# Stacked key halves from block 2 on, and block 0's first products of slices 8 to 15 from split weights and split tokens

## The chip, the cores and the metric

The kernel runs on one core of a Trainium2 chip. The metric is the device time of one execution in microseconds; before the change the median of three runs is 1127.58 us (1126.95 to 1127.78). The engines are TensorE (PE; its weight loads are listed as PEld), VectorE (DVE), ScalarE (ACT), GpSimd (POOL) and SyncE (SP), which issues most transfers. A difference of 0.2%, about 2.25 us, is the least that the measurement tells from no change.

## The reference

Three stages follow each other. Attention with 4 sink keys and a window of 128 (4 batches, 8 heads, 768 positions, 64 wide) gives 3072 tokens of 512 numbers. A dense layer pair follows, and then a mixture of 8 experts in which every token goes to its best one.

```python
x = attn_out.transpose(0, 2, 1, 3).reshape(B * S, H * D)   # 3072 x 512
h = np.maximum(x @ w_in, 0.0)                               # w_in 512 x 2048
x = h * h @ w_out                                           # w_out 2048 x 512
...
e_idx = np.argmax(x @ w_gate, axis=1)
for e in range(E):
    mask = e_idx == e
    h = np.maximum(x[mask] @ w1[e], 0.0)
    out[mask] = gate_w[mask, None] * eom[mask, e, None] * (h @ w2[e])
```

The weights of the dense pair come as float64.

## The kernel before, in words

The 3072 tokens are worked in 12 blocks of 256 (t = 0 to 11). For each block PE makes the dense pair in 16 slices of 128 hidden units (j): `l1(t, j)` is a slice's first product, from the tokens `x` and the weights `WI`, and `l2(t, j)` its second, into two accumulators. Between the two, ACT takes the positive part (line 692), POOL (block 0) or DVE squares it (line 699), ACT makes a high part of the square (line 701) and DVE the low part (line 702). The attention of block t + 1 is worked among the slices of block t, so that PE always has something to do; its pieces are `prep_k`, `prep_q` (transposed keys and queries), `scores`, `ptrans`, `pv` (weights times values), `fin_sink` and `add_sink` (the sink keys' share). Behind block 11 comes the expert stage.

Products of float32 numbers are made in one of two ways. In plain float32 the operands are used as they are. In the split way each operand is a high part in the reduced format fp32r and a low part (the rest), and three products high·high, high·low, low·high stand for one. A split costs an ACT copy for the high part and a DVE subtraction for the low part; `fin()` in `conv` does it for weights (lines 340 and 341).

Weights of the dense pair arrive as float64 in slabs of 512 KB, one for each slice of w_in and one for each slice of w_out, in turn. There are three slab buffers. `conv` turns a slab into float32: two passes on ACT (lines 327 and 330) and two on DVE (lines 336 and 337); the end of DVE's second pass frees the slab buffer, and SP issues the next load. The float32 slice (`fw`) lies in the place that the low part of the split slice will have. In block 0 the weights are still coming in: there the first products of all 16 slices, and the second products of slices 0 to 7, are plain float32 from `fw` (lines 682 and 711), and the split of those slices (`fins`) follows once they were used, by the rule of `LAGS` 12 or 13 slices later at the latest. `cstep` in the loop over slices starts the conversions ahead of the slices that need them.

`scores` works in three forms. Blocks 0 and 1 use plain float32 (line 521). Block 2 uses split queries and keys as three products for each of the two heads of a pair, each on 64 of the 128 rows (line 528), six in all. From block 3 on the keys are stacked: a head's high part on one half of the rows and its low part on the other, so that two products on all 128 rows do (line 524), four in all. For that `prep_k` and `prep_q` write each head's half by itself (lines 423, 425, 470, 472) and POOL copies query halves (line 474). The constant `STK` is the first block in the stacked form, `T32` the first in a split form.

The order of each engine's instructions is fixed when the kernel is built, by a scheduler that goes by program order, by priorities (`tc.high_priority`) and by its own estimates of durations; at run time each engine works through its list in order and waits on semaphores. `psH`, `psX`, `psS`, `psT`, `psO` are the pools of accumulators.

In the tables below psh is a first product's accumulator, psx a second product's, pss a unit of scores, pspt and PT its transposed probabilities, pso the product with the values, psst and psk the sink share, xT the split tokens, craw a slab, fw a float32 slice, h and r the hidden units.

## Time and profile before

| | us |
|---|---|
| median of 3 runs | 1127.58 |
| the profiled execution, its own time | 1127.6 |
| its span | 1125.9 |
| PE busy | 1103.8 (98%) |
| DVE busy | 777.6 (69%) |
| ACT busy | 667.6 (59%) |
| POOL busy | 448.9 (40%) |

The time of an execution is about 1.7 us longer than the span, which runs from the first to the last instruction. Busy shares are means over stages that differ: block 0 lies between about 38 and 123 us, block 1 ends at about 190 us, the dense pair ends at about 762 us, and the expert stage fills the rest. PE's ends are modelled and its instructions overlap, so the time that a group of products takes is read from the start of its first one to the start of what follows. An idle time in brackets names who released the engine.

### The profile page before, as it was taken

Reading aid. Unit: us, or ns where it says so; the run is one execution under the profiler, and the core shown is the slowest. Engines: PE = TensorE matmul, PEld = TensorE weight load, DVE = VectorE, ACT = ScalarE, POOL = GpSimd, SP = SyncE. Lnnn points to the kernel's source line nnn. Section 1 sums busy time; section 2 is a strip of 40 time slices with the busy share of each in tenths; the row PEclk is TensorE's granted clock in tenths of the full one; section 3 lists DMA queues with packets and bytes.
Section 4 is the critical chain, followed back from the end, with each engine's and each line's share of the span. In section 5 each row is a group of like instructions: output and inputs, shape, how many; then the busy total and the mean of one; then the engine's idle time right before and its main releaser. Section 6 shows DMA issues by size and latency. Waiting matters only on the chain. (4 is left out here: it accounts for less than half of the span.)

```text
span 1125.9 us, 23911 instructions
## 1 busy us (share of the span) xinstructions
PE 1103.8 (98%) x6858; PEld 938.7 (83%) x6858; DVE 777.6 (69%) x2094; ACT 667.6 (59%) x1821; POOL 448.9 (40%) x997
## 2 busy tenths in 40 slices
PE   9999999999999999999999999999999999999997
PEld 5556788989999989999988999997788888888886
DVE  6799877788887778787778787567412576864144
ACT  6788777778787878787877777454222222222200
POOL 3234564356664436576336665210211222221121
PEclk9999999999999999999999999999999999999999
DMA  6676211121111111211111110394411456654111
GB/s 163 181 219 196 72 26 49 40 56 37 52 29 50 39 49 35 57 30 48 39 51 38 39 32 2 60 233 158 132 39 48 162 178 227 218 193 153 48 46 34
DMA packets 139329, 100.09 MB, mean 89 GB/s; under 512 B 103843, under 2 KB 112163, under 8 KB 139174
## 3 DMA queue, kind: packets, MB, share of 16 engines
q1 hardware_dynamic: 131604, 83.19, 26.5%
q0 software_dynamic: 5408, 14.19, 3.7%
q8 instruction: 63, 1.03, 0.4%
q10 hardware_dynamic: 2162, 0.92, 0.3%
q14 instruction: 92, 0.75, 0.3%
HBM read 85.56 MB, written 13.76 MB: 88 GB/s over the span
## 5 line engine op out<-in xcount | busy, mean ns | idle before, releaser
L690 PE MATMUL psh<-xT,WI 128*128 128x256 f32 x2112 | 283.9, 283 | 0.6 <-ACT xT L649 0.6
L690 PEld LDWEIGHTS psh<-xT,WI 128*128 128x128 f32 x2112 | 265.7, 188 | 8.8 <-ACT xT L649 0.8
L1032 PE MATMUL psh<-WI,xt 128*128 (+1 forms) x672 | 162.1, 395 | 1.0 <-ACT xt L1012 0.7
L714 PE MATMUL psx<-WOb,h 128*128 128x512 f32 x576 | 151.4, 398 | 1.3 <-ACT h L701 0.9
L1032 PEld LDWEIGHTS psh<-WI,xt 128*128 128x128 f32 x672 | 123.8, 188 | 26.7 <-ACT xt L1012 1.4
L714 PE MATMUL psx<-WOa,h 128*128 128x512 f32 x528 | 139.0, 398 | 0.0
L699 DVE TENSOR_TENSOR r<-r 128x256 f32<-128x256 f32 x176 | 90.5, 515 | 59.5 <-ACT r L692 58.1
L1048 DVE TENSOR_TENSOR ht<-psht,ht 128x512 fp32r<-128x512 f32 x56 | 38.5, 689 | 120.8 <-ACT ht L1012 120.4
L714 PEld LDWEIGHTS psx<-WOb,h 128*128 128x128 f32 x576 | 101.6, 188 | 20.7 <-ACT h L701 2.3
L701 ACT ACTIVATE h<-r 128x256 fp32r<-128x256 f32 x184 | 76.3, 415 | 61.0 <-DVE r L699 54.7
L714 PEld LDWEIGHTS psx<-WOa,h 128*128 128x128 f32 x528 | 92.8, 188 | 15.1
L1070 POOL DMA_INDIRECT out_dram<-xg,pidx x28 | 29.4, 1049 | 190.4 <-ACT xg L1069 132.9
L702 DVE TENSOR_TENSOR h<-r,h 128x256 fp32r<-128x256 f32 x184 | 83.1, 451 | 23.1 <-ACT h L701 20.6
L581 POOL TENSOR_SCALAR_AFFINE_SELECT PT<-PT 128x256 fp32r<-128x256 f32 x224 | 96.8, 465 | 2.2 <-PE pss L528 1.2
L536 ACT ACTIVATE P<-P,st 128x260 f32<-128x260 f32 (+1 forms) x192 | 92.6, 485 | 7.0 <-DMA vn<-in_v_dram 3.5
L692 ACT ACTIVATE r<-psh 128x256 f32<-128x256 f32 x192 | 72.8, 379 | 34.2 <-PE psh L690 28.9
L1038 ACT ACTIVATE r<-psh 128x512 f32<-128x512 f32 x48 | 28.8, 599 | 98.8 <-PE psh L1032 94.5
L1061 PE MATMUL psy<-WOb,ht 128*128 (+1 forms) x336 | 84.0, 398 | 0.0
L617 POOL TENSOR_TENSOR xr<-tB,tC 128x128 f32<-128x128 f32 x80 | 37.0, 462 | 114.5 <-DVE tB L616 74.6
L1061 PE MATMUL psy<-WOa,ht 128*128 (+1 forms) x336 | 82.2, 392 | 0.0
L1003 POOL DMA_INDIRECT xg<-x2tab,pidx x30 | 42.2, 1407 | 90.7 <-issue 50.0
L533 DVE CUSTOM_DVE_ANT_0 P<-pss,M 128x260 f32<-128x260 f32 (+1 forms) x184 | 68.4, 398 | 10.6 <-POOL V L480 3.3
(459 smaller groups left out, 2108.5 us busy)
## 6 DMA issues: line engine op xcount, KB each, us to landing
raw<-in_moe_w_dram SPq DMA_DIRECT2D x36, 1024.0 KB
craw<-in_moe_w_out_dram SPq DMA_DIRECT2D x15, 512.0 KB
craw<-in_moe_w_in_dram SPq DMA_DIRECT2D x14, 512.0 KB
x2tab<-x2s SPq DMA_DIRECT2D x24, 256.5 KB
kn<-in_k_dram SPq DMA_DIRECT2D x64, 96.0 KB
vn<-in_v_dram SPq DMA_DIRECT2D x64, 96.0 KB
qn<-in_q_dram SPq DMA_DIRECT2D x92, 64.0 KB
kn<-in_k_dram SPq DMA_DIRECT2D x32, 64.0 KB
```

Of the source, the lines that this page charges most:

```text
L533: V.tensor_tensor_reduce(out=P[:, e, 0:W], in0=ps[e][:, 0:W], in1=mask[:, 0:W], scale=-SCALE, scalar=3.0e38, op0=ALU.add, op1=ALU.min, acc ...
L536: exps.append(A.activation(out=P[:, e, 0:W], in_=P[:, e, 0:W], func=AF.Exp, scale=-1.0, bias=st[:, e:e + 1], accum_out=st[:, 4 + e:5 + e]))
L581: G.affine_select(out=both[:, 1 - b, e], in_=bf[:, 0, e], pattern=[[0, 2], [1 - 2 * b, 128]], compare_op=ALU.is_gt if b else ALU.is_ge, fi ...
L690: PE.matmul(ps[:], lhsT=WI[:, j, a_, kk, :], rhs=x[:, b_, kk, :], start=(n == 0), stop=(n == 11))
L692: A.activation(out=hq[:], in_=ps[:], func=AF.Relu)
L699: E_.tensor_tensor(out=hq[:], in0=hq[:], in1=hq[:], op=ALU.mult)
L701: A.activation(out=o[:, 0], in_=hq[:], func=AF.Copy)
L702: V.tensor_tensor(out=o[:, 1], in0=hq[:], in1=o[:, 0].bitcast(F32), op=ALU.subtract)
L714: PE.matmul(acc[t][m][:], lhsT=o[:, a_, 128 * m:128 * m + 128], rhs=WO[j // 8][:, j % 8, b_, :], start=(j == 0 and n == 0), stop=(j == NF ...
L1003: G.indirect_dma_start(out=x, out_offset=None, in_=x2tab[:] if s >= PRE else x2tab[0:256 * (NBLK - 3)], in_offset=bass.IndirectOffsetOnAxi ...
L1032: PE.matmul(ps[:], lhsT=o[:, a_, kk, :], rhs=wview(n, par + 2048 * b_ + 512 * kk, 512), start=(c == 0), stop=(c == 11))
L1061: PE.matmul(yp[s][:], lhsT=o[:, a_, kk, :], rhs=wview(2 + n, par + 2048 * b_ + 512 * kk, 512), start=(n == 0 and kk == 0 and c == 0), stop ...
```

## The change

There are three parts, and some that follow from them.

1. `STK` goes from 3 to 2: block 2's scores take the stacked form. Its keys and queries are prepared by halves, its accumulators come from the pools of the stacked form, `fin_sink(2)` gets its later place, and the unused middle form stays in the text. The sink keys' halves (`sk`) are now laid out stacked and made in `prep_k(1, p)` from the plain copy `sk32`.
2. `NAT1 = 8`: in block 0 the first products of slices 0 to 7 stay plain float32 (four products a slice, each two instructions in the trace), and those of slices 8 to 15 become split products, twelve a slice. Weight slices 8 to 15 are split at once behind their conversion.
3. For that, block 0's tokens are split too, in front of slice 3: four ACT copies and four DVE subtractions. The parts (`x0`) lie where the high parts of weight slices 4 to 7 will come, so the splits of those four slices follow only behind slice 15.

```diff
--- before.py
+++ after.py
@@ -30,7 +30,7 @@
 HOME = 224
 REG = NT + 128
 XW = 513
-T32, STK = 2, 3
+T32, STK = 2, 2
 HALF = (slice(0, 64), slice(64, 128))
 
 
@@ -42,6 +42,7 @@
 NSLOT = NT // 128 + NE - 1
 PRE = 2
 LAGS = (12, 13)
+NAT1 = 8
 
 
 @with_exitstack
@@ -339,10 +340,10 @@
             def fin():
                 A.activation(out=hi, in_=f, func=AF.Copy)
                 x = V.tensor_tensor(out=lo, in0=f, in1=hi.bitcast(F32), op=ALU.subtract)
-                if n < len(fw):
+                if n in used:
                     after(x, used[n])
 
-            if n < len(fw):
+            if n < NAT1 or NF <= n < len(fw):
                 fins[n] = fin
             else:
                 fin()
@@ -358,6 +359,7 @@
     gx = moe.tile([128, 2048], F32, name="gx", tag="xT", bufs=1)
     moe.tile([128, HOME // 4], F32, name="gap1", bufs=1)
     xTs = {}
+    x0 = []
 
     got = set()
 
@@ -406,13 +408,16 @@
             kf = kv[:, 0].bitcast(F32)
             V.tensor_copy(out=kf[:, o:3, 0:128], in_=ps[:, o:3])
             if o:
-                G.tensor_copy(out=sk[:, p, 0], in_=kf[:, 1, 0:NS])
-                G.tensor_tensor(out=sk[:, p, 1], in0=kf[:, 1, 0:NS], in1=sk[:, p, 0].bitcast(F32), op=ALU.subtract)
                 G.tensor_copy(out=sk32[:, p], in_=kf[:, 1, 0:NS])
             for n in range(o, 2):
                 x_ = G.tensor_copy(out=kf[:, n, 128:KS], in_=sk32[:, p])
             if t == 0 and p == 1:
                 skd.append(x_)
+            if t == 1:
+                for e in range(2):
+                    G.tensor_copy(out=sk[HALF[e], p, e], in_=sk32[HALF[e], p])
+                    G.tensor_tensor(out=sk[HALF[1 - e], p, e], in0=sk32[HALF[e], p], in1=sk[HALF[e], p, e].bitcast(F32),
+                                    op=ALU.subtract)
             kTt[t, p] = kt
             return
         if t < STK:
@@ -641,6 +646,8 @@
             SY.dma_start(out=xr[:] if t else xT0[:],
                          in_=xtab[H * b:H * b + H, :, 256 * u:256 * u + 256].rearrange("(p e) d s -> (e d) p s", e=2))
         if t == 0:
+            for a_ in range(2):
+                x0.append([WI[:, 4 + 2 * a_ + kk // 2, 0].rearrange("p k f -> p (k f)")[:, 256 * (kk % 2):256 * (kk % 2) + 256] for kk in range(4)])
             return
         if t == 1:
             xTs[0] = moe.tile([128, 2, 4, 256], F32R, name="xT", tag="xT", bufs=1)
@@ -677,7 +684,7 @@
     def l1(t, j):
         ps = psH.tile([128, 256], F32, tag="h", name="psh")
         x = xTs.get(0)
-        if t == 0:
+        if t == 0 and j < NAT1:
             for kk in range(4):
                 used[j] = PE.matmul(ps[:], lhsT=fw[j][:, 128 * kk:128 * kk + 128], rhs=xT0[:, kk, :], start=(kk == 0), stop=(kk == 3))
         else:
@@ -687,7 +694,7 @@
             if t == 1 and j == 0:
                 fill(ps[:], 4)
             for n, (kk, a_, b_) in enumerate(terms):
-                PE.matmul(ps[:], lhsT=WI[:, j, a_, kk, :], rhs=x[:, b_, kk, :], start=(n == 0), stop=(n == 11))
+                PE.matmul(ps[:], lhsT=WI[:, j, a_, kk, :], rhs=x[:, b_, kk, :] if t else x0[b_][kk], start=(n == 0), stop=(n == 11))
         hq = moe.tile([128, 256], F32, tag="r", name="r", bufs=2)
         A.activation(out=hq[:], in_=ps[:], func=AF.Relu)
         E_ = G if t == 0 else V
@@ -1093,6 +1100,10 @@
             pc, half = SPLITS[j]
             split_raw(pc, 4096 * half, True)
             load_raw(pc, es[half + 1], True)
+        if t == 0 and j == 3:
+            for kk in range(4):
+                A.activation(out=x0[0][kk], in_=xT0[:, kk], func=AF.Copy)
+                V.tensor_tensor(out=x0[1][kk], in0=xT0[:, kk], in1=x0[0][kk].bitcast(F32), op=ALU.subtract)
         if t == 0:
             cstep(max(2 * j + 3, 17 + j) - st_["done"])
         for n0, lag in zip((0, NF), LAGS):
```

On PE the first place is slice 15 of block 0, the last whose weights come in (`fw_70` is its float32 slice, psx_1285/1286 before and psx_1293/1294 after are block 0's second accumulators). Before:

```order
L714 MATMUL psx_1285<-WOb,h_1776 128x512
L714 MATMUL psx_1286<-WOb,h_1776 128x512
L565 MATMUL pspt<-ident,P 128x128
L635 MATMUL pso_1863<-pskT,vsk 128x256 x2
L714 MATMUL psx_1285<-WOb,h_1776 128x512 x2
L682 MATMUL psh<-xT_591,fw_70 128x256 x3
L640 COMPARE_AND_BRANCH
L640 UNCONDITIONAL_BRANCH x2
L682 MATMUL psh<-xT_591,fw_70 128x256
L714 MATMUL psx_1286<-WOb,h_1776 128x512 x2
L442 MATMUL psq<-ident,qn 128x128 x2
```

After the change, the same place:

```order
L529 MATMUL pss_1759<-kT,qst 128x260 x2
L529 MATMUL pss_1760<-kT,qst 128x260
L697 MATMUL psh<-WI 128x256 x2
L721 MATMUL psx_1293<-WOb,h_1872 128x512 x2
L721 MATMUL psx_1294<-WOb,h_1872 128x512
L404 MATMUL psk__1827<-ident,kn 128x128 x3
L721 MATMUL psx_1294<-WOb,h_1872 128x512
L529 MATMUL pss_1882<-kT,qst 128x260 x2
L721 MATMUL psx_1294<-WOb,h_1872 128x512
L697 MATMUL psh<-WI 128x256 x10
```

The slice's eight instructions in four rows are now twelve; two of them, which need no low part, stand ahead, and second products, three key transposes of block 2 and two stacked scores of block 2 have moved between them and the other ten.

On DVE the second place is the conversion of that same slice; before, line 337 on `fw_70` is what the products of slice 15 need:

```order
L336 SCALAR_TENSOR_TENSOR fw_70<-craw 128x512
L420 TENSOR_TENSOR kT<-psk__1743,kT 128x3x128
L341 TENSOR_TENSOR WOb<-fbuf,WOb 128x512
L702 TENSOR_TENSOR h_1776<-r,h_1776 128x256
L337 SCALAR_TENSOR_TENSOR fw_70<-craw,fw_70 128x512
L533 ISA P,st<-pss_1785,M_137 128x260
L533 ISA st 128x1
L636 TENSOR_TENSOR xr<-pso_1863,xr 128x512
```

After the change they need line 342 on `fw_70` (line 341 before):

```order
L337 SCALAR_TENSOR_TENSOR fw_70<-craw 128x512
L477 TENSOR_TENSOR qst<-psq,qst 64x256
L338 SCALAR_TENSOR_TENSOR fw_70<-craw,fw_70 128x512
L477 TENSOR_TENSOR qst<-psq,qst 64x256
L709 TENSOR_TENSOR h_1872<-r,h_1872 128x256
L337 SCALAR_TENSOR_TENSOR fbuf<-craw 128x512
L538 ISA P,st<-pss_1759,M_137 128x260
L538 ISA st 128x1
L538 ISA P,st<-pss_1760,M_137 128x260
L538 ISA st 128x1
L342 TENSOR_TENSOR WI<-fw_70,WI 128x512
```

Behind the second pass there are now five rows (query half, hidden units, the next slab's first pass and two units' maxima) and then the low part of the slice itself.

The third place, also on DVE, is the split of block 1's tokens (xT, line 650 before and 657 after) that opens block 1. Before:

```order
L337 SCALAR_TENSOR_TENSOR fbuf<-craw,fbuf 128x512
L538 TENSOR_SCALAR st<-st 128x2
L650 TENSOR_TENSOR xT<-xr,xT 128x256
L702 TENSOR_TENSOR h_1860<-r,h_1860 128x256
L539 RECIPROCAL st<-st 128x2
L542 TENSOR_TENSOR P<-P 128x2x128
L341 TENSOR_TENSOR WOb<-fbuf,WOb 128x512
L650 TENSOR_TENSOR xT<-xr,xT 128x256 x3
L577 TENSOR_TENSOR PT<-pspt,PT 128x2x128
```

After the change:

```order
L641 TENSOR_TENSOR xr<-pso_1969,xr 128x512
L709 TENSOR_TENSOR h_1966<-r,h_1966 128x256
L645 COMPARE_AND_BRANCH
L645 UNCONDITIONAL_BRANCH x2
L543 TENSOR_SCALAR st<-st 128x2
L547 TENSOR_TENSOR P<-P 128x2x128
L544 RECIPROCAL st<-st 128x2
L342 TENSOR_TENSOR WI<-fw_59,WI 128x512
L657 TENSOR_TENSOR xT<-xr,xT 128x256 x3
L582 TENSOR_TENSOR PT<-pspt,PT 128x2x128
L657 TENSOR_TENSOR xT<-xr,xT 128x256
```

The sums and the reciprocal of one more unit and the low part of weight slice 4 (`fw_59`) now stand ahead of the token split, and the splits of w_out and hidden units that stood among its parts stand further ahead.

## Rows read from the trace of the kernel before

**Rows 1.** Busy us (x instructions) of each engine in three stretches, clock, DMA:
```profile
38.60:60.00 21.40, 20.84 (x93) 12.07 (x91) 15.13 (x39) 15.95 (x37) 7.20 (x18) 1.00 0.67 201
60.00:120.50 60.50, 57.52 (x258) 36.62 (x257) 55.64 (x115) 51.86 (x117) 24.05 (x42) 1.00 0.71 204
120.50:131.20 10.70, 10.02 (x58) 8.36 (x59) 9.59 (x27) 7.98 (x23) 3.76 (x11) 1.00 0.11 26
```

**Rows 2.** Waits of PE, 38.6 to 156 us: us in total, times, longest:
```profile
PE psst L627 <- POOL psk L553: 1.4, 1, 1.4
PE psh L682 <- DVE fw L337: 0.7, 2, 0.5
```

**Rows 3.** PE timeline, block 0: start us, us, [idle before <-releaser]:
```profile
77.00 1.89 PE L682 MATMUL psh<-xT,fw 128*128 128x256 f32 x8
78.82 0.65 PE L599 MATMUL pso<-PT,vn 128*64 128x128 f32 x4
88.64 1.94 PE L682 MATMUL psh<-xT,fw 128*128 128x256 f32 x8
94.23 1.99 PE L682 MATMUL psh<-xT,fw 128*128 128x256 f32 x8 [0.24 <-DVE fw L337]
120.54 1.99 PE L682 MATMUL psh<-xT,fw 128*128 128x256 f32 x8 [0.49 <-DVE fw L337]
131.22 1.56 PE L690 MATMUL psh<-xT,WI 128*128 128x256 f32 x12
```

**Rows 4.** DVE timeline, block 0: three second weight passes and block 1's token split:
```profile
87.85 0.68 DVE L337 SCALAR_TENSOR_TENSOR fw<-craw,fw 128x512 int32<-128x512 int32 x1
93.34 0.83 DVE L337 SCALAR_TENSOR_TENSOR fw<-craw,fw 128x512 int32<-128x512 int32 x1
119.40 1.09 DVE L337 SCALAR_TENSOR_TENSOR fw<-craw,fw 128x512 int32<-128x512 int32 x1
125.98 1.09 DVE L650 TENSOR_TENSOR xT<-xr,xT 128x256 fp32r<-128x256 f32 x3
```

**Rows 5.** PE timeline, block 2: a slice's first products, and what follows it:
```profile
208.78 1.56 PE L690 MATMUL psh<-xT,WI 128*128 128x256 f32 x12
210.19 0.63 PE L607 MATMUL pso<-PT,V 128*128 128x256 f32 x4
```

**Rows 6.** PE timeline, a unit of scores in block 1, one in block 2:
```profile
142.29 0.64 PE L607 MATMUL pso<-PT,V 128*128 128x256 f32 x4
142.85 0.63 PE L528 MATMUL pss<-kT,qT 64*128 64x260 f32 x6
143.41 0.44 PE L565 MATMUL pspt<-ident,P 128*128 128x128 f32 x2
143.61 1.64 PE L714 MATMUL psx<-WOa,h 128*128 128x512 f32 x6
195.83 0.63 PE L607 MATMUL pso<-PT,V 128*128 128x256 f32 x4
197.00 1.56 PE L714 MATMUL psx<-WOa,h 128*128 128x512 f32 x6
```

**Rows 7.** Waits of DVE, 60 to 120.5 us:
```profile
DVE P L533 <- PE pspt L565: 1.1, 2, 0.9
DVE h L702 <- ACT h L701: 1.1, 1, 1.1
DVE P L533 <- PE pss L528: 0.6, 1, 0.6
DVE WOa L341 <- PE psx L711: 0.6, 1, 0.6
```

**Rows 8.** Lines 340, 341, 425: ns min/median/max, first and last start:
```profile
L340 ACT ACTIVATE WI<-fw x16: 612/622/633, 24.8 to 120.5; 128x512 fp32r<-128x512 f32 x16
L341 DVE TENSOR_TENSOR WI<-fw,WI x16: 662/686/894, 40.6 to 140.2; 128x512 fp32r<-128x512 f32 x16
L425 DVE TENSOR_TENSOR kT<-psk__3391,kT x2: 551/556/560, 223.2 to 223.8; 64x384 fp32r<-64x384 f32 x2
```

## The prediction, made before the changed kernel was run

> **What bounds the kernel now.** I read the table of stretches first. From 38.6 to 120.5 us block 0 runs; PE is busy 57.52 of the 60.5 us from 60 on, DVE 55.64, ACT 51.86, all at a granted clock of 1.00 [rows 1]. So PE leads, but DVE follows closely: it does the second half of every weight conversion. The waits of PE come next, and they are small: 1.4 us on one sink product, 0.7 us on weights (fw) in two waits [rows 2]. Small waits are not the whole story, and the timelines of PE and DVE laid side by side show why. The second pass over slice 10 (line 337) runs from 87.85 to 88.53, and PE starts that slice's products at 88.64; slice 11: done at 94.17, started at 94.23, after an idle 0.24; slice 15: done at 120.49, started at 120.54, after an idle 0.49 [rows 3, 4]. PE's queue holds just enough other work to arrive when the weights do. Two things therefore end block 0 together: PE's own work, and the stream of weights through ACT and DVE. The reader should expect that work taken from PE alone comes back partly as waiting.
>
> **What goes from PE.** Slice 8 in plain float32 takes eight PE instructions from 77.00 until the next operation at 78.82, 1.82 us [rows 3]. Twelve reduced-precision products of the same size take from 208.78 to 210.19, 1.41 us [rows 5]. Eight slices at 0.41 us give 3.3 us. A unit of scores (one head pair, 128 queries) with the four P·V products before it and the transposes behind it takes 142.29 to 143.61, 1.32 us, in block 1, and 195.83 to 197.00, 1.17 us, where it is stacked [rows 6]. Attention tile 2 has eight units: 8 × 0.15 = 1.2 us. Together 4.5 us less on PE, all inside blocks 0 and 1; from about 175 us on the order of every engine is the same in both kernels, and a gain before it moves the rest forward as a whole.
>
> The trace times the six unstacked score products at 142.85 to 143.41, 0.56 us, 0.093 us each [rows 6]. The Trainium skill (TensorEngine Tiling (Array Packing), Theoretical Speedup) says that a contraction of 64 rows or less can run up to twice as fast, since two row halves work side by side. By it six would take three slots, 3 × 0.117 = 0.35 us at the rate of rows 5, and stacking would lose 0.21 us a unit; the trace does not agree, as 0.56 us is nearer to six slots than to three.
>
> **What is added on ACT and DVE.** Up to the row that completes slice 15 (the second pass before, the low part now), the order of DVE has four token subtractions (0.36 each, from 1.09 for three [rows 4]), one more raw pass (0.69) and one more query half (0.36): 2.5 us. Two splits of w_out (0.69 each), one addition and two small ones, some 1.9 us, now stand behind it. The splits of slices 8 to 15 replace those of slices 4 to 7, which wait until the tokens in their places are read, in equal numbers (twelve up to that row in both). Net +0.6 us. ACT has four splits of 0.62 us [rows 8] fewer there and four shorter copies more: no cost, DVE hides it.
>
> Each of the slices 8 to 15 gets a hand-over: DVE's second pass, ACT's high part (0.62), DVE's low part (0.69) [rows 8]. What is queued behind the waiting low part on DVE is the next slab's pass, whose end also frees a slab buffer for the next load on SP; so a wait here holds up the next slice as well. In the order one raw pass (0.69) stands between the two DVE steps as cover, in slice 15 five rows. The cost lies between 0 (cover holds) and 0.69 + 0.62 per slice; I take near 0, since 0.69 covers 0.62.
>
> Against this DVE gains where it waited for PE: 1.1 for pspt, 0.6 for pss, 0.6 for psx, and 1.1 for h, which comes from PE through ACT and POOL: 3.4 us from 60 to 120.5 [rows 7]. If all of it goes, slice 15 is complete 3.4 − 0.6 = 2.8 us earlier; if none goes, 0.6 later. I take a little under half, 1.6 − 0.6 = 1.0 us earlier, since PE's head start grows only slice by slice.
>
> **The sum.** PE reaches slice 15 by 7 × 0.41 = 2.9 us earlier, the weights are there 1.0 us earlier: 1.9 us of new waiting. Then comes the start of block 1. Before, from 120.49 to the last token part at 125.98 + 1.09 = 127.07, 6.6 us pass [rows 4], and PE is at the third slice at 131.22 [rows 3]. In the new order DVE has two key halves (0.56 each, rows 8), three small rows of one more unit (about 0.5, an estimate from 0.36 for the addition) and a transposed P (0.36) more ahead of the last token part, and one raw pass (0.69) less: 0.8 to 1.3 us later after the weights; and slice 15's own products, the cover, are 0.41 us shorter. That is 1.2 us more of waiting. So 4.5 − 1.9 − 1.2 = 1.4 us of gain. The rest costs nothing: POOL's eight query copies and eight small sink operations lie beside 36 us in which POOL idles (24.05 busy of 60.5 [rows 1]); if that cover is gone, the price is one more wait like the 1.4 us on psst [rows 2]. SP issues the same loads; those of block 2's keys and queries shift a few places, and slab loads wait for DVE's second pass in both, so they go with it. The late splits of slices 4 to 7 are needed only from slice 4 of block 1.
>
> The profiled execution took 1127.6 us (span 1125.9 and 1.7 around it), the median of the three runs is 1127.58: the sum carries over unchanged, 1127.6 − 1.4 = 1126.2.
>
> **Rivals.** (1) PE alone is the bound. If DVE follows fully (2.8 us) and the token split's delay stays covered, the gain is between 4.5 − 0.1 − 1.2 = 3.2 and 4.4 us, 1123.2 to 1124.4. For it: PE's busy share, above DVE's. Against it: three starts within 0.11 us of their weights.
> (2) Slower: the hand-over. ACT is busy 51.86 of 60.5 us [rows 1], and its two raw passes for the next slab can stand ahead of the high part, so that DVE waits, slab buffers come free later and the whole stream slips. At 0.5 us a slice, 8 × 0.5 = 4.0 us take the place of 1.0 us of lead: slice 15 comes 3.0 us later, and 1.4 − 4.0 = −2.6, 1130.2. It counts as slower from about 0.46 us a slice. For it: slices 9 to 15 lean on the stream already. Against it: the raw pass as cover.
> (3) The change does not do what it says for the scores: row halves that ran side by side are lost. By the rule above 0.21 us a unit is lost where 0.15 us was won, 8 × 0.36 = 2.9 us, which gives 1129.1. Against it: the stacked unit is shorter in this very trace [rows 6].
>
> **How the numbers follow.** About 0.2%, 2.25 us, is what a measurement of this kernel can tell from no change. Forecast 0.42, its own range 1124.4 to 1127.8 (slice 15 from 2.8 us earlier to 0.6 later); rival 1 0.34, rival 2 0.16, rival 3 0.08. Faster than 1125.3: 0.32 of rival 1 and 0.05 of the forecast, 0.37. Slower than 1129.8: 0.15 of rival 2, 0.01 each of rival 3 and the forecast, 0.17. The rest, 0.46, is no change. The range runs from rival 1's far end to the middle of rival 2: 1123.2 to 1130.2.
>
> **What would show it.** Right: PE's time per slice 8 to 15 falls from 1.82 to about 1.41; PE waits on WI (low part, line 342) of about 2 us in all before slice 15; slice 15's low part done near 119.5; token wait of PE at the start of block 1 up by about a microsecond; score units in block 1 near 1.17. Rival 1: no such waits, DVE busy above 95% from 60 us on. Rival 2: DVE rows of line 342 with idle time released by ACT, slice 15 after 122 us. The forecast is wrong if PE's waits in block 0 stay at their old size, or if the difference arises after 175 us.

## The result, and the profile after

The changed kernel is slower: 1133.58 us, median of 6 runs (1132.56 to 1136.17), against 1127.47 us (6 runs); the ratio is 1.0057, 95% interval 1.0047 to 1.0068. I had forecast 1126.2, with a range up to 1130.2. Measured again beside the experiments (e11_again below) the ratio was 1.0053 (1.0037 to 1.0068).

Where the time arises is read from one operation that both kernels have once per weight slice: ACT's relu of the slice's first product (line 692 before, 699 after). Its starts in us, slice (block, number), from ACT's timelines; "again" is the same changed program in a second profile:

| | (0,0) | (0,12) | (0,15) | (1,3) | (1,8) | (2,0) |
|---|---|---|---|---|---|---|
| before | 40.61 | 103.85 | 122.57 | 139.91 | 157.76 | 193.21 |
| changed | 40.83 | 101.08 | 124.72 | 141.20 | 164.09 | 199.02 |
| again | 40.91 | 101.37 | 123.75 | 140.22 | 163.13 | 198.24 |
| e1_products | 40.35 | 104.27 | 123.64 | 141.57 | 160.02 | 195.47 |
| e2_stack | 40.41 | 102.19 | 125.51 | 141.73 | 162.89 | 197.48 |
| f1_pt | 40.62 | 104.12 | 125.31 | 141.77 | 163.84 | 198.12 |
| f4_ptq | 41.00 | 104.39 | 124.77 | 142.79 | 162.42 | 196.71 |
| h1_chain | 40.81 | 101.25 | 123.87 | 143.08 | 162.06 | 196.04 |
| f5_as_unstacked | 40.68 | 101.13 | 124.94 | 142.85 | 162.68 | 197.38 |

Counted from (0,0), the changed kernel is 3.0 us ahead at slice (0,12), 1.1 behind at (1,3), and 5.6 behind at the start of block 2; after that the difference grows little. Only the last of these marks compares the same work. At (2,0) PE has done in both kernels all that stands ahead of it. At (0,12) the changed kernel has put off eight products with the values, two query transposes and a sink product, some 1.4 us (an estimate from 0.14 us a product and 0.10 a transpose in [rows 6]), and its five split slices so far can save 5 × 0.41 = 2.05 us at most; e2_stack, which has no split products, is 1.5 us ahead there too. At (1,3) some 1.1 us (estimated in the same way) of work are still put off. So the lead at (0,12) is not all saving, and part of what seems lost in block 1 is work that comes later.

From (0,0) to (2,0), before, changed and "again", with the columns of [rows 1]:

```profile
40.61:193.21 152.60, 146.03 (x829) 108.34 (x830) 126.81 (x330) 119.62 (x313) 69.52 (x149) 1.00 0.43 122
40.83:199.02 158.19, 142.17 (x845) 108.99 (x846) 131.02 (x339) 123.01 (x321) 67.26 (x158) 0.99 0.41 117
40.91:198.24 157.33, 140.94 (x845) 107.96 (x846) 131.27 (x339) 122.72 (x322) 67.54 (x158) 1.00 0.41 118
```

At full clock ("again") PE is 5.1 us less busy than before, a little more than the 4.5 us forecast. But it is not busy for 16.4 us, where it was for 6.6. PE's work shrank as planned; 9.8 us of new waiting came in its place.

The stretches of the changed kernel, with the columns of [rows 1]; the third is the middle of block 1:

```profile
60.00:120.50 60.50, 52.66 (x266) 35.47 (x264) 53.63 (x107) 50.02 (x111) 18.77 (x38) 0.97 0.64 192
120.50:131.20 10.70, 8.25 (x52) 6.46 (x52) 9.88 (x30) 9.56 (x28) 3.72 (x12) 1.00 0.19 43
140.00:158.00 18.00, 15.14 (x96) 12.92 (x95) 14.87 (x42) 12.18 (x36) 11.42 (x27) 1.00 0.10 23
```

The same middle of block 1 in the kernel before:

```profile
140.00:158.00 18.00, 17.91 (x126) 15.88 (x124) 12.84 (x36) 12.69 (x38) 11.53 (x27) 1.00 0.15 33
```

Up to 120.5 PE is 4.9 us less busy than in [rows 1], and the granted clock is 0.97 instead of 1.00. In block 1 PE, which was busy 17.91 of 18 us, is busy 15.14. No engine has become full: ACT and POOL do as much as before, DVE 2.0 us more. So PE waits. The changed kernel's largest waits of PE from 60 to 124 us, and the largest from 124 to 165 us, answer to [rows 2]:

```profile
PE psst L632 <- POOL psk L558: 2.0, 1, 2.0
PE psh L697 <- ACT WI L341: 1.7, 2, 1.3
...
PE pso L612 <- POOL PT L586: 3.7, 4, 1.4
PE pss L529 <- DVE qst L477: 0.7, 1, 0.7
```

In the kernel before the line for PT, from 124 to 165 us, reads:

```profile
PE pso L607 <- POOL PT L581: 1.1, 2, 0.9
```

PT is what P·V multiplies in a stacked unit: POOL makes it by four masked copies of the transposed P. POOL's timeline of the changed kernel at one of them, and PE's:

```profile
144.32 0.77 POOL L586 TENSOR_SCALAR_AFFINE_SELECT PT<-PT 128x256 fp32r<-128x256 f32 x2 [0.34 <-DVE PT L582]
145.03 0.68 POOL L556 CAST psk<-P 128x8 fp32r<-128x8 f32 x1
145.66 0.66 POOL L557 CAST psk<-P 128x8 fp32r<-128x8 f32 x1
146.27 0.61 POOL L586 TENSOR_SCALAR_AFFINE_SELECT PT<-PT 128x256 fp32r<-128x256 f32 x1
146.84 0.20 POOL L558 TENSOR_TENSOR psk<-P,psk 128x8 fp32r<-128x8 f32 x1
147.00 0.41 POOL L586 TENSOR_SCALAR_AFFINE_SELECT PT<-PT 128x256 fp32r<-128x256 f32 x1
...
146.93 1.03 PE L612 MATMUL pso<-PT,V 128*128 128x256 f32 x4 [1.38 <-POOL PT L586]
```

Two of the four copies stand behind small copies (psk) of another unit that nobody wants yet. In the kernel before the four stand together, 1.4 us ahead of PE:

```profile
146.76 1.74 POOL L581 TENSOR_SCALAR_AFFINE_SELECT PT<-PT 128x256 fp32r<-128x256 f32 x4 [0.27 <-DVE PT L577]
148.46 0.18 POOL L551 CAST psk<-P 128x8 fp32r<-128x8 f32 x1
...
149.92 0.64 PE L607 MATMUL pso<-PT,V 128*128 128x256 f32 x4
```

### The profile page after: what moved, and what is told of

It reads as the page before. It is cut to its first block, busy times and chain, and to the rows that moved or that the text cites. A ratio compares the mean times of both kernels' runs of the same rounds, so it can differ in the third digit from the quotient of the medians.

```text
span 1132.1 us, 24009 instructions
## 1 busy us (share of the span) xinstructions
PE 1100.6 (97%) x6874; PEld 939.6 (83%) x6874; DVE 784.4 (69%) x2106; ACT 671.9 (59%) x1833; POOL 443.7 (39%) x1013
## 5 line engine op out<-in xcount | busy, mean ns | idle before, releaser
L1055 DVE TENSOR_TENSOR ht<-psht,ht 128x512 fp32r<-128x512 f32 x56 | 38.5, 689 | 121.0 <-ACT ht L1019 120.5
L553 ACT ACTIVATE P<-P,st 128x132 f32<-128x132 f32 (+2 forms) x168 | 62.2, 415 | 19.8 <-DVE st L544 16.1
```

Source lines behind the costliest of these rows:

```text
L553: A.activation(out=P[:, e, 0:W], in_=P[:, e, 0:W], func=AF.Copy, scale=st[:, 6 + e:7 + e])
```

## The experiments

Ratios are to the kernel before on the same chip, with 95% intervals; 0.001 is 1.13 us. Line numbers in rows are each kernel's own.

**Each half of the change alone.** e1_products keeps the split products, e2_stack the stacked tile:

```diff
# e1_products (the keys of the first four tokens, sk, are made as before as well)
-T32, STK = 2, 2
+T32, STK = 2, 3
# e2_stack (no token parts for block 0)
-NAT1 = 8
+NAT1 = 16
```

> The split first products of slices 8 to 15 alone; attention tile 2 as before. Theory H (the hand-over of split weights, my second rival: DVE's second pass, ACT's high part, DVE's low part make the weights of slice 15 late): this part carries the loss, 1131 to 1134 us, slice 15's low part after 121 us. Theory S (the stacked tile 2 carries the loss, through the copies and halves that it adds on POOL, ACT and DVE in slices 11 to 15 and in block 1): 1124 to 1127 us here, since the products save 3.3 us on PE and only some of it comes back as waiting.

> The stacked tile 2 alone; the first products of slices 8 to 15 as before. Theory H: 1126 to 1128 us, since 1.2 us of score products go and little comes in. Theory S: 1131 to 1135 us, with PE waiting for POOL's masked copies of P (PT) in block 1 for 3 us or more, where the kernel before waits 1.1 us. If both parts are near 1127.5 by themselves, the loss is in their meeting (split weights that are late only because the halves of tile 2 stand in the same queues).

Measured: e1_products 1.0026 (1.0012 to 1.0040), e2_stack 1.0044 (1.0024 to 1.0064). Both halves lose by themselves, and the sum, 1.0070, is not far from the whole. On the 1127.47 us of the first measurement e1_products is 1130.4 us, just below the range of theory H and far above that of theory S; e2_stack is 1132.4, in the range of theory S. So each theory is right about the half that it blames and wrong about the other; which half is larger, the intervals don't tell. The mark that theory S named failed: PE waits 1.4 us for PT in e2_stack from 124 to 165 us, not 3. In e1_products it is 1.3. The 3.7 us of the changed kernel arise only where the two halves meet.

What e1_products loses stands in its profile as waits of PE for h, the high part of the squares, from 38.6 to 124 us; the kernel before, then e1_products:

```profile
PE psx L714 <- ACT h L701: 0.5, 1, 0.5
PE psx L718 <- ACT h L705: 5.4, 4, 2.7
```

No edit here takes this wait alone away, so that it is the cause is read from the profile, not tested. What the stacked tile does in e2_stack can be seen at the sink product (psst): DVE's P, ACT's query halves, POOL and PE, in that order:

```profile
105.82 0.34 DVE L551 TENSOR_SCALAR P<-P,st 128x260 f32<-128x260 f32 x1
106.91 0.77 ACT L475 ACTIVATE qst<-psq 64x256 fp32r<-64x256 f32 x2
107.40 1.59 POOL L479 CAST qst<-qst 64x256 fp32r<-64x256 f32 x2 [3.86 <-ACT qst L475]
109.05 0.19 POOL L556 CAST psk<-P 128x8 fp32r<-128x8 f32 x1
109.59 0.33 PE L632 MATMUL psst<-ident,psk 128*128 128x128 f32 x1 [2.68 <-POOL psk L558]
```

P is ready at 106.16 us and POOL stands idle until 107.40, and yet psk starts at 109.05: the query copies are ahead of it in POOL's queue, and the first of them waits for ACT. PE pays 2.68 us.

**Is it the clock?** e3_fill puts idle matmuls where PE paused, in the changed kernel; e7_hold does so in e1_products:

```diff
# e3_fill, in fin_sink (for tile 1)
+                fill(ps[:].rearrange("p n c -> p (n c)"), 10)
# e7_hold, in l1, into the unused half of the same PSUM tile
+        if t == 0 and j in (12, 14):
+            fill(pw[:, 256:512], 10)
```

> The changed kernel, with ten idle matmuls of 512 columns on PE ahead of the transposes of tile 1's sink probabilities (psst), where PE stood idle for 2.04 us and the granted clock then fell to 0.50 for about 3 us. Theory C (a long pause of PE costs twice: the pause, and then work at half clock): no 0.50 in block 0, and 1.5 us less than the changed kernel, 1131 to 1132.5 us against 1133.6 on the same footing (before 1127.5). Theory S (the wait itself is the loss and the clock is only a companion, since PE waits again soon after): same time as the changed kernel within 0.5 us, the clock held or not.

> The split first products alone (as in e1_products), with ten idle matmuls of 256 columns (some 1.5 us) on PE behind the products of slice 12 and ten behind those of slice 14, ahead of the two pauses after which the granted clock fell to 0.50. Theory C (the loss of e1_products is the clock: two stretches of 3 to 4 us at 0.50 cost 3.5 us of PE work): fewer such stretches up to 131 us, and the ratio falls from 1.0026 to 1.000 or below. Theory W (the waits for h and for the weights are the loss, and PE would wait for them at any clock): ratio 1.002 to 1.004, since the idle matmuls add work and bring nothing sooner.

Measured: e3_fill 1.0049 (1.0033 to 1.0065), e7_hold 1.0030 (1.0018 to 1.0042). e3_fill is not told apart from the changed kernel; its profile has no stretch at a granted clock of 0.50 (the lower of the two levels, 1.2 against 2.4 GHz) in block 0, but one from 127 to 131 us behind another pause of PE (1.7 us for WOb). Nor is it a test of the clock alone: in its trace rows of all engines have changed places between about 100 and 172 us. In e7_hold's profile there is no stretch at 0.50 from 60 to 200 us, and the timed runs are as in e1_products, as theory W had it; in that one profile, though, e7_hold is only 0.2 us behind the kernel before at (2,0), where e1_products is 2.5. The cleanest answer came unasked, from e11_again: the same program, the same pause (psst, 2.04 us in both), once with the clock falling behind it and once without. The changed kernel, and then "again", same columns:

```profile
112.00:113.00 1.00, 1.00 (x6) 0.99 (x5) 1.00 (x2) 1.00 (x3) 0.00 (x0) 0.50 0.85 319
113.00:114.00 1.00, 1.00 (x8) 1.00 (x6) 0.78 (x3) 0.94 (x2) 0.00 (x0) 0.50 0.28 111
114.00:115.00 1.00, 1.00 (x5) 0.81 (x4) 1.00 (x2) 0.66 (x2) 0.00 (x0) 0.50 0.00 0
```
```profile
112.00:113.00 1.00, 0.95 (x7) 0.58 (x6) 1.00 (x3) 1.00 (x3) 0.37 (x1) 1.00 0.94 270
113.00:114.00 1.00, 1.00 (x9) 0.94 (x8) 1.00 (x2) 1.00 (x3) 0.00 (x0) 1.00 0.51 205
114.00:115.00 1.00, 1.00 (x9) 0.93 (x8) 0.74 (x3) 1.00 (x3) 0.00 (x0) 1.00 0.00 0
```

At (1,3) the two are 1.1 us apart (from (0,0): 100.37 and 99.31), at (2,0) 0.9. That is the price of this fall, in one pair of profiles. Without it "again" is still 4.7 us behind the kernel before at (2,0). In the changed kernel the clock is a companion; for e1_products see below.

> The changed kernel once more, unedited, as the reference on the chip of this call for the edits beside it. 1.0047 to 1.0068 of the kernel before, as measured first.

**The weight stream and the end of block 0.** e4_sqdve takes squares off POOL, e6_last3 takes the hand-over from the last three slices, e9_slabs mends SP's queue, e10_before_fill adds PE work to the kernel before:

```diff
# e4_sqdve
-        E_ = G if t == 0 else V
+        E_ = G if t == 0 and j < 12 else V
# e6_last3 (and the same range where the splits are put off)
-        if t == 0 and j < NAT1:
+        if t == 0 and not NAT1 <= j < 13:
# e9_slabs, in loads (V of head pair 2 is issued one pair later too)
+                if nm == "v" and t == 2 and p >= 2:
+                    behind(x_, slabs[-1])
# e10_before_fill: the kernel before, with e7_hold's lines
```

> The changed kernel, with the squares of block 0's slices 12 to 15 on DVE instead of POOL. Theory P (POOL's queue is the loss: the square stands behind V halves and sink copies, ACT's high part of h waits for it, and behind that stand the high parts of the weights and the raw passes): the low part of slice 15 comes at 120 us or before instead of 121.9, and the time falls by 2 to 4 us, to 1130 to 1132. Theory H (the hand-over of the weights through the two in-order queues is late whatever POOL does): under 1 us of gain, since DVE gets four operations of 0.4 us more.

> The changed kernel, with slices 13 to 15 back in float32 (no hand-over where the queues are fullest), slices 8 to 12 split. Theory H: slice 15's products start when DVE's second pass is done, near 118 to 119 us instead of 122, and the time falls by 3 us or more, to 1129 to 1130.5. Theory S: the stacked tile 2 goes on costing 4 to 5 us, and the time stays at 1132 or above.

> The changed kernel, with the loads of V for the last two head pairs of tile 2 issued behind the last weight slab. In the changed kernel SP stood at one of them from 99.7 to 105.1 us, until POOL's half of V had freed its place, with two slab loads behind it. Theory Q (SP's queue holds up the slabs, and so the raw passes, the hand-over of slice 13 and P of tile 1's last unit): DVE's wait of 1.6 us at 105 us for craw goes, slice 13's low part comes before 105.5 us instead of 106.5, PE's wait of 2.0 us for psst shrinks, and the ratio falls by 0.002 or more against the unedited changed kernel. Theory P (the wait for craw comes from ACT, which stands at the square on POOL, not from the load): the loads are earlier and nothing else is, ratio as the unedited kernel.

> The kernel before, with the twenty idle matmuls of e7_hold at the same places (3.0 us of PE work added). If PE bounds the end of block 0 as it stands: 1.0027 (3.0 us). If it has slack there, so that what is taken from PE comes back as waiting: 1.001 or less, and then the 3.3 us that the split products take from PE could never have been worth more than that either.

Measured: e4_sqdve 1.0060 (1.0047 to 1.0073), e6_last3 1.0081 (1.0068 to 1.0095), e9_slabs 1.0040 (1.0024 to 1.0056), e10_before_fill 1.0011 (0.9998 to 1.0023). Squares on DVE bring nothing. Slices 13 to 15 in float32 make it worse, against theory H, so a return to float32 there does not win the hand-over back; its profile has three stretches at 0.50, and how much of the rest is their doing is not separated. e9_slabs is better by 1.5 us in the timed runs, which the intervals don't separate, and in its profile PE's wait for psst is still 2.1 us and it is 4.5 us behind at (2,0) ("again" 4.7): theory Q is not borne out. e10_before_fill shows slack: about 3 us of added work cost 1.2 (−0.2 to 2.6).

**POOL's queue.** e5_qact and e8_stack_qact (the same edit in e2_stack) take the eight query copies off POOL; f1_pt raises the masked copies; f4_ptq does both in the changed kernel, g1_stack_mended both in e2_stack; e12_both is e5_qact with e9_slabs; h1_chain is f4_ptq with the two steps ahead of the masked copies raised as well; g2_before_pt is f1_pt's edit in the kernel before:

```diff
# e5_qact, e8_stack_qact, e12_both, f4_ptq, g1_stack_mended, h1_chain: in prep_q, tile 2
-                G.tensor_copy(out=o[HALF[1 - e], 0, e], in_=o[HALF[e], 0, e].bitcast(F32))
+                    A.activation(out=o[HALF[1 - e], 0, e], in_=ps[HALF[e], 0:2], func=AF.Copy)
# f1_pt, f4_ptq, g1_stack_mended, g2_before_pt, h1_chain: in ptrans, around G.affine_select
+            with (tc.high_priority(100) if t == 2 else ExitStack()):
# h1_chain: the same around the A.activation and V.tensor_tensor ahead of it
```

> The changed kernel, with the query halves of tile 2 copied a second time from PSUM by ACT instead of from SBUF by POOL (eight copies of 0.4 to 0.6 us leave POOL, eight of 0.37 go to ACT). Theory P: POOL's masked copies of P in block 1 come earlier, PE's wait for them falls from 3.7 us to near the 1.1 us of the kernel before, and the time falls by 2 us or more, to 1131.5 or less. Theory A (ACT is the queue that all hand-overs pass): no gain or slower, 1133.5 to 1136.

> The stacked tile 2 alone (as in e2_stack), with the eight query copies on ACT, straight from PSUM, instead of on POOL. In e2_stack the copies of the sink probabilities stood on POOL behind two query copies that waited for ACT, P was ready at 106.2 us and PE got the copies at 109.6 us. Theory P (order on POOL's queue): PE's wait for psst falls from 2.7 us to 1.5 us or less, no stretch at 0.50 follows it, and the ratio falls from 1.0044 to 1.002 or below. Theory A (ACT's queue): ACT's late copies are still late, the wait moves to the scores (pss), and the ratio stays at 1.004 or above.

> The edit of e9_slabs together with the query copies of tile 2 on ACT (as in e5_qact). If the two causes add up: below either alone, 1.001 to 1.003. If they are the same delay seen twice: as the better of the two alone. It would beat the kernel before only if the stacked scores and the split products were then worth their 4.5 us of PE.

> The changed kernel, with tile 2's four masked copies of P (PT) put ahead of the small copies on POOL; only POOL's order differs, 22 rows of it. In the unedited kernel the third and fourth copy stand behind the sink copies and the query copies, and PE waits 3.7 us for them at the start of block 1. Theory P (order on POOL's queue sets block 1): that wait falls to about 1 us, the slices (1,3) to (1,8), between which 5 us are lost, lose 2 us or less, ratio 1.003 or below. Theory U (one unit's whole chain through DVE, ACT and POOL is longer than the two slices that PE has to do meanwhile): the wait moves to the next step of the chain (tB, scores, transposes) and the ratio stays at 1.005.

> Both edits for POOL: the masked copies of P first, and the query copies on ACT. Theory P: 1.002 or below, PE's waits in block 1 as in the kernel before. Theory U: 1.003 to 1.005, as with the query copies on ACT alone, since ACT and DVE stand in the same chain.

> The changed kernel with both edits for POOL (as in f4_ptq, 1.0017), and the two steps ahead of the masked copies, P's high half on ACT and its low half on DVE, raised in priority for tile 2 as well. In the changed kernel DVE's half of one unit started 3.0 us after ACT's, behind seven other operations. If the order on DVE is the rest of the chain: PE's waits for PT in block 1 go below 1 us and the ratio to 1.000 to 1.001. If not (what it overtakes is wanted as soon): 1.002 or more.

> The stacked tile 2 alone (as in e2_stack, 1.0044), with both edits for POOL: query copies on ACT and masked copies of P first. If POOL's queue is what the stacking cost: 1.0005 or below, near or below the kernel before, since 1.2 us of score products are then saved (f4_ptq less e1_products: 1.0017 - 1.0026, about 1 us below the kernel before). If ACT's and DVE's halves cost as much: 1.002 to 1.003, as with the query copies on ACT alone (1.0025).

> The kernel before with the masked copies of P first on POOL, as a control. PE waits 1.1 us for them there in block 1, so at most 1 us can be gained: 0.999 to 1.000. If it gained 2 us or more, the gain of f1_pt would not be the mending of what the stacking did.

| | ratio | 95% interval | behind at (2,0), us | PE not busy, us | at 0.50, us |
|---|---|---|---|---|---|
| before | 1 | | 0 | 6.6 | 0 |
| changed, again | 1.0057, 1.0053 | 1.0047–1.0068, 1.0037–1.0068 | 5.6, 4.7 | 16.0, 16.4 | 3.4, 0 |
| f1_pt | 1.0024 | 1.0009–1.0039 | 4.9 | 14.0 | 6.8 |
| f4_ptq | 1.0017 | 1.0006–1.0027 | 3.1 | 11.9 | 6.8 |
| h1_chain | 1.0019 | 1.0008–1.0031 | 2.6 | 13.1 | 3.4 |
| e5_qact | 1.0037 | 1.0024–1.0050 | 1.9 | 13.7 | 0 |
| e12_both | 1.0053 | 1.0033–1.0073 | 3.8 | 13.3 | 6.8 |
| e2_stack | 1.0044 | 1.0024–1.0064 | 4.5 | 11.2 | 6.8 |
| e8_stack_qact | 1.0025 | 1.0011–1.0039 | 2.6 | 10.4 | 3.4 |
| g1_stack_mended | 1.0037 | 1.0024–1.0050 | 2.2 | 10.7 | 3.4 |
| g2_before_pt | 0.9992 | 0.9981–1.0003 | −1.0 | 5.7 | 0 |

The last three columns are of each kernel's one profile, counted from (0,0) to (2,0); the last is the length of the stretches at 0.50. A profile can have such stretches where the timed runs have others, so the ratios decide.

f1_pt is the run that decides. It moves 22 rows of POOL's order, from 145 us on, and not one of any other engine, and takes 3.3 us off the timed ratio of "again". POOL and PE at the place shown above, in f1_pt:

```profile
145.24 2.43 POOL L587 TENSOR_SCALAR_AFFINE_SELECT PT<-PT 128x256 fp32r<-128x256 f32 x4 [0.34 <-DVE PT L582]
147.62 0.37 POOL L556 CAST psk<-P 128x8 fp32r<-128x8 f32 x1
...
146.91 0.50 PE L613 MATMUL pso<-PT,V 128*128 128x256 f32 x2 [0.44 <-POOL PT L587]
147.72 0.51 PE L613 MATMUL pso<-PT,V 128*128 128x256 f32 x2 [0.31 <-POOL PT L587]
```

The four copies are together again, and 1.38 us of waiting has become 0.75. Theory P's other marks are met in part: PE's waits for PT from 124 to 165 us go from 3.7 to 2.7 us, not to 1, and (1,3) to (1,8) still loses 4.2 us of 5.0. The size of the gain is less sure than its sign: the interval of f1_pt ends below the first one of the changed kernel, but overlaps the second by a hair (1.0037 to 1.0039). The clock does not make it: the mean granted clock of the timed runs is 0.9975 in f1_pt and 0.9973 and 0.9962 in the two sets of the changed kernel. f1_pt's own profile does not show the gain in its total, 4.9 us behind at (2,0) between 5.6 and 4.7. It fell into 6.8 us at 0.50 in block 0, where its orders are still those of the changed kernel: at (1,3) it is 1.8 us later than "again". From there to (2,0) it loses 3.1 us, the two unedited profiles 4.5 and 4.7, and PE's time without work is 2.0 to 2.4 us shorter.

With the query copies moved too (f4_ptq) the timed ratio falls to 1.0017, clear of both intervals of the changed kernel. The middle of block 1 in f1_pt, f4_ptq and h1_chain, against 15.14 and 17.91 us of busy PE above (the same stretch of time, not of work: f4_ptq and h1_chain come to (1,3) 1.6 and 1.9 us later than the changed kernel):

```profile
140.00:158.00 18.00, 16.12 (x101) 13.63 (x100) 16.34 (x43) 13.01 (x38) 11.45 (x28) 1.00 0.10 23
```
```profile
140.00:158.00 18.00, 16.47 (x104) 13.67 (x104) 17.25 (x47) 15.35 (x49) 10.63 (x28) 1.00 0.10 24
```
```profile
140.00:158.00 18.00, 16.91 (x114) 14.70 (x115) 16.93 (x48) 15.10 (x48) 13.14 (x30) 1.00 0.16 36
```

PE fills up step by step as the chain ahead of P·V is put in order, and h1_chain's wait for PT is 0.6 us. But its total is not better than f4_ptq's, and it lies between the two forecasts made for it. Misses: e5_qact, 1.0037, is just above theory P's bound (1131.6 us on the first measurement, 1131.5 named), and PE's wait for PT there is 2.6 us, not 1.1; f4_ptq meets the ratio that theory P named, but PE still waits 2.2 us for PT; e8_stack_qact brought 2.1 us of the 2.7 expected, which the intervals don't separate from e2_stack, and PE's wait moved to the sink product (2.1 us for pskT from ACT), so theories P and A are both half right there; g1_stack_mended should have reached 1.0005 and is apart from neither e2_stack nor e8_stack_qact, so for the stacked half alone no edit of POOL's order is shown to help (its wait for PT was 1.4 us to begin with); e12_both came out as the unedited kernel, though each of its edits alone had come out lower. g2_before_pt gains 0.9 us (−0.3 to 2.1) in the kernel before from the same order: little enough for f1_pt's gain to be mostly a mending, though the intervals do not exclude an overlap.

**Bank and priority.** Tile 2 gets another PSUM tile for its keys, another for its sink product and a raised priority by the same condition (`t < STK`). f5_as_unstacked gives these back (and by the same edit the sink product's tile and place in the order, not shown):

```diff
-        if t < STK:
+        if t < 3:
             ps = psT.tile([128, 4, 128], F32, tag="T", name="psk_")
-        with (tc.high_priority(100) if t >= STK else ExitStack()):
+        with (tc.high_priority(100) if t >= 3 else ExitStack()):
```

> The changed kernel, with tile 2 stacked in its arithmetic alone: its key transposes go back to the PSUM tile that it had before (psT, not the first one of the scores), its sink transposes too, and its score reductions have no raised priority. Theory B (the bank: keys in the scores' tile make scores wait for both key halves, and the raised priority puts the reductions ahead of weight work): ratio falls by 0.002 or more, to 1.0035 or below. Theory P or U: within 0.001 of the unedited kernel (1.0053).

Measured: 1.0053 (1.0036 to 1.0070), as the changed kernel, so the gain that theory B forecast is not there. The run is also a caution. The scheduler moved rows of all engines with this edit and put three of the first four groups of masked copies together; PE's wait for PT from 124 to 165 us is 1.2 us, and from (1,3) to (2,0) only 1.2 us are lost. Yet the time is that of the changed kernel: it is 2.9 us behind at (1,3) already, its profile has 10.2 us at 0.50, and the mean clock of its timed runs is 0.9932. Masked copies in good order are not enough by themselves. No kernel that holds any part of the change beat the kernel before.

## Why the prediction was wrong

**Right: the work on PE.** The forecast took 4.5 us from PE; "again" is 5.1 less busy up to (2,0). Ten of a split slice's twelve products take 1.20 us at full clock (slice 15 of the changed kernel, 122.08 to 123.28), so twelve take a little over 1.4 where eight instructions of float32 took 1.82 [rows 3]. A stacked unit takes 1.10 us where 1.17 was forecast. PE's rows for both, the changed kernel, then "again":

```profile
122.08 1.35 PE L697 MATMUL psh<-WI 128*128 128x256 f32 x10
123.28 0.61 PE L106 MATMUL psh<-idle 128*128 128x256 bf16 x4
```
```profile
162.84 0.64 PE L612 MATMUL pso<-PT,V 128*128 128x256 f32 x4
163.31 0.65 PE L529 MATMUL pss<-kT,qst 128*128 128x260 f32 x4
163.80 0.38 PE L570 MATMUL pspt<-ident,P 128*128 128x128 f32 x2
163.94 1.63 PE L721 MATMUL psx<-WOa,h 128*128 128x512 f32 x6
```

**Wrong: the waits.** The sum gave back 1.9 and 1.2 us; measured are 9.8 us of new time without work. Of the two terms one is there: PE's waits for WI, forecast near 2 us, are 1.7 for the high parts and 0.4 for the low (the forecast had them on the low part). The other is not: PE waited 0.6 us for the tokens (xT) in the kernel before, and in the changed one not at all. For h, which PE needs for a slice's second products, the sum has no term; it is 1.3 to 1.6 us against 0.5, and 5.4 in e1_products. For e1_products, the split products alone, the forecast's terms are 3.3 saved and 3.1 given back, 0.2 faster; it is 2.9 us slower.

**Wrong in size: the hand-over.** I took it near 0 a slice beyond the 1.31 us of its two halves. From the end of the second pass to the end of the low part it takes 2.1 us in slice 8 and 5.7 in slice 15. The chain of slice 15 in the changed kernel, DVE, POOL, ACT:

```profile
115.51 0.67 DVE L338 SCALAR_TENSOR_TENSOR fw<-craw,fw 128x512 int32<-128x512 int32 x1
117.42 0.35 POOL L485 CAST V<-vn 128x192 fp32r<-128x192 f32 x1 [5.47 <-PE pso L604]
117.73 0.61 POOL L706 TENSOR_TENSOR r<-r 128x256 f32<-128x256 f32 x1
118.38 0.42 ACT L708 ACTIVATE h<-r 128x256 fp32r<-128x256 f32 x1 [0.30 <-POOL r L706]
118.70 0.62 ACT L341 ACTIVATE WI<-fw 128x512 fp32r<-128x512 f32 x1
118.83 0.63 DVE L709 TENSOR_TENSOR h<-r,h 128x256 fp32r<-128x256 f32 x1 [2.18 <-ACT h L708]
121.20 0.69 DVE L342 TENSOR_TENSOR WI<-fw,WI 128x512 fp32r<-128x512 f32 x1
```

The second pass ended at 116.18, 4.3 us earlier than in [rows 4], and the low part at 121.89, 1.4 us later than the weights were complete before. I had forecast 1.0 us earlier, 119.5; 2.4 us are missing in the sum (in "again", without the clock's fall, the low part ends at 120.93 and 1.4 are missing). The high part stood on ACT behind an h whose square stood on POOL behind a copy that waited for PE, and the low part on DVE behind that h, a raw pass and the maxima of two units. Rival 2 had this mechanism, with the high part late on ACT, at 4.0 us more than the forecast; 2.4 came, or 1.4. Its mark (slice 15 after 122 us) is met by PE's start at 122.08, but not in "again" (121.12); the idle time that it looked for at line 342 stands at the h (line 709, 2.18 us).

**Wrong: the stacked tile.** The step that failed is "The rest costs nothing: POOL's eight query copies and eight small sink operations lie beside 36 us in which POOL idles [...]; if that cover is gone, the price is one more wait like the 1.4 us on psst." I read POOL's busy time from the stretch before 120.5 us, but 26 of tile 2's 32 score products run from 124 us on, where POOL is busy 11.4 of 18 us; and idle time is no cover in a queue that keeps its order. The Trainium skill (TensorE: Matmul & The Clock Gate, the table at its head) calls the queues of ScalarE, VectorE and GpSimdE strict FIFO. The trace agrees: in e2_stack psk waited 2.9 us behind two query copies, while POOL did nothing for 1.2 of them. So 1.2 us of gain on the scores became a loss: e2_stack, which is this part alone, is 5.0 us slower. The price I had set was one wait of 1.4. In the changed kernel the waits for psst and PT alone came to 2.0 and 3.7 us, against 1.4 and 1.1 before; the order of 22 rows on POOL is worth 3.3 us of its time (f1_pt), and with the query copies off POOL some 4 (f4_ptq, 1.0053 to 1.0017). That this step failed is shown by these edits; why f4_ptq is still 1.9 us slower than the kernel before (0.7 to 3.1) is not.

**Not in the prediction: the clock.** I looked at the granted clock, found 1.00 and went on. Waits that I costed at their own length can be followed by a stretch at 0.50; the one in the changed kernel cost 0.9 to 1.1 us.

**Rival 3** (row halves that run side by side are lost) is out. In "again" P·V starts at 162.84 and the weights' second products at 163.94: a stacked unit in block 1 takes 1.10 us where nothing is waited for, against 1.32 in [rows 6]. The Trainium skill (TensorEngine Tiling (Array Packing), Theoretical Speedup) gives products of at most 64 rows up to twice the speed, by which the unstacked halves would have been the quicker form. The trace shows less: an unstacked product takes 0.093 us [rows 6], a stacked one 0.12 (four from 163.31 to 163.80 in "again"), 1.3 times and not twice, so that four of these are quicker than six of those. The price that I gave this rival was also miscounted: four stacked products at 0.117 are 0.47 us, so that by the estimate from the page stacking would lose 0.12 us a unit, not 0.21.

**Open.** Why e1_products is 2.9 us slower (1.3 to 4.5). Its waits for h would do it, but its profile also has 6.8 us at 0.50, and the mean granted clock of its 12 timed runs is 0.9949, of the kernel before 0.9974 (18 runs). In e7_hold the clock is 0.9973 against 0.9978 and the time the same, but there about 3 us of idle matmuls had been added, which cost the kernel before 1.2. A lower mean clock does not turn into time one for one: the changed kernel has nearly the same ratio at 0.9973 and 0.9962, and f5_as_unstacked at 0.9932. Clock and waits can't be parted by these runs. Nor can the runs say why g1_stack_mended is not better than e8_stack_qact, whose order it shares but for 21 rows of POOL and 2 of PE.

## What to carry to other kernels

Work that is moved to an engine with idle time is free only if nothing that another engine wants soon stands behind it in that engine's queue: ask what each new instruction waits for and what is queued behind it, in every stretch in which it runs, not in the one where the change is most visible. Where a helper engine makes the operand of the bound engine's next step, put that first in its queue and the bookkeeping behind it. And cost a change of one engine's work by the whole chain: here 5 us were won on PE, seen in the trace, and 10 given back wherever PE then stood waiting, for weights, for h and for masked copies. To see both, compare two kernels at a mark by which PE has done the same work in each.

## What the runs showed that I had not expected

- One program, one pause of 2.04 us on PE, two outcomes: granted clock 0.50 for some 3.5 us behind it, or 1.00 throughout. Pauses of 1.6 and 2.7 us (e2_stack, at 154 and 109 us) were followed by 0.50, as was one of 1.4 us in f1_pt; one of 2.1 us in e9_slabs was not.
- In the one pair of profiles that differ by it, a stretch of some 3.5 us at 0.50 cost about 1 us, less than the 1.7 us of full-clock work that it takes away. That PE was to wait for others anyway would explain it; it is not shown.
- The same small instruction on POOL (psk, 128x8) takes 0.18 us in one place and 0.92 in another (e1_products, at 107.45 us), and the square of 128x256 took 0.61 us or 1.62 (e1_products, at 115.77 us), as the profile has them; POOL's spans in it are rough.
